# Three-stage attention and two-layer feed-forward kernel: third product's partial sum copied out by ScalarE, decode slots and late jobs moved

## The chip, the cores and the metric

One core of one Trainium2 chip runs the whole program. The metric is device time in microseconds of one execution; lower is better. Engines in the rows: PE is TensorE (PEld its weight loads), DVE is VectorE, ACT is ScalarE, POOL is GpSimd, SP is SyncE, which issues the DMAs.

## The reference, cut to what matters

```
attention, B=8 H=8 S=576 D=64, in chunks of 64:
    p = softmax(q_c @ k_c.T / 8);  x = p @ v_c            -> x [4608, 512]
layer 1:  h = relu(x @ w_in);   g = s*h*h + b;   y   = g @ w_out        (512 -> 2048 -> 512)
layer 2:  h = y @ w2_in;  g = (a0+a1 h+a2 h^2+a3 h^3) / (1+|b0||h|+|b1|h^2+1e-6);  out = g @ w2_out
```

The weights reach the kernel as 64-bit floats and are decoded on the chip.

## The kernel before

The 36 tiles of 128 tokens form ten blocks: 0 and 1 of two tiles, 2 to 9 of four (512 tokens). Blocks 2 to 9 of layer 1 and nine blocks of layer 2 hold nearly all of the time. Every operand is split into a high and a low fp16 half, and a product takes three matmuls (high by high, high by low, low by high).

**Layer 1, blocks 2 to 9** (`l1_group`). A block has four groups, u = 0 to 3, and a group four slots, so a block has 16. A group makes seven products of a fast 2x2 block multiplication ("1", "7", "2", "6", "4", "5", "3", 12 matmuls each, L446) into two PSUM banks called Z and Y, and between them the second matrix product of the group before (`m2(0)` to `m2(3)`, L485) and attention work of the next block. After "4" and "5", Y and Z hold partial sums to which the saved product 7 (`p7`) is added: DVE adds Y+p7 (L519) and Z+p7 (L520) into the tile `h1`. Then ACT makes Relu (L522), Square (L492) and an fp16 copy (L493) of `h1`, and DVE its low half (L494), which is the `g` that the next group's `m2(0)` reads. Product "3" goes on into Z, and ACT reads Z at L527. The next group takes the two banks the other way round: its product 1 goes into the bank that was Y, its product 7 into the one that was Z.

**Other work of a block.** Attention for the next block (scores L264, exponentials, P times V L312, eviction L316 into the single tile `x32`), the seven pieces of x (`x_piece`, L415 on ACT and L416 on DVE), the norm and the seven pieces of y of the block before (`y_norm`, `y_piece`). Scores and P times V share a PSUM bank, so a score waits for the eviction L316 before it, and L316 waits until the last piece of the old `x32` is made.

**Weights of layer 2** are decoded during layer 1 (`w2_load`, `w2_park`): 16 loads of two units each; one unit is three bit operations on DVE (L142, L144, L145), a maximum (L587) and a store to DRAM. `w2_scale` then reduces the maxima over all partitions on POOL and makes the scales; `l2_par(j)` makes the coefficients of layer 2's block j by some twenty one-column DVE operations.

**What sets the order.** `at(slot, job)` gives each job a slot; `run_jobs` issues a slot's jobs inside the group. A scheduling layer then orders the instructions of each engine by readiness and priority, so a job may stand earlier than its slot says. Each engine works its queue in that order.

**Layer 2** is 36 groups; group i makes products into PSUM, group i-1's rational function runs on DVE and ACT (`chain_a` to `chain_e`), and group i-2's second product on PE (L989). `late_jobs` spreads what is left of layer 1 (norm and pieces of the last y block, the last splits of w2_out) over the first groups.

Of the kernel before, what the change touches and what calls it, by code (L numbers as in the profile page):

```python
# [12 lines left out]
AF = mybir.ActivationFunctionType  # L13
ALU = mybir.AluOpType
# [6 lines left out]
def attn_moe_moe2(ctx: ExitStack, tc: tile.TileContext, qk, v, w_in, w_out, s_in, b_in,  # L21
                  w2_in, w2_out, a2_in, b2_in, out):
    nc = tc.nc
# [414 lines left out]
    def product(w, x, u, p, b, start, stop=False):  # L438
        wk, pk = PROD[p]
        for s in range(2):  # L440
            f = 2 * u + s
            for kk in range(2):
                t = w.sh[wk, kk, f // 4]
                for n, (a, l) in enumerate(TERMS):
                    o = (f % 4) * 128
                    T.matmul(out=b[:, s, :], lhsT=t[:, a, o:o + 128], rhs=x[pk][:, l, kk, :],  # L446
                             start=start and s + kk + n == 0, stop=stop and s + kk + n == 4,
                             skip_group_check=True)
# [41 lines left out]
    def l1_half(h, g):  # L490
        hf = h.rearrange("p s b t -> p (s b t)")
        A.activation(out=hf, in_=hf, func=AF.Square)  # L492
        A.activation(out=g[:, 0], in_=hf, func=AF.Copy)  # L493
        V.tensor_tensor(out=g[:, 1], in0=hf, in1=g[:, 0], op=ALU.subtract)  # L494

    def l1_group(j, u, jobs_at, m2):
        x = xhl[j]
        bank = lambda nm: ps_h.tile([128, 2, 256], F32, name=nm, tag="h")
        half = lambda: l1_p.tile([128, 2, 2, 256], F32, name="h1", tag="h1")
        jobs_at(0, crit.get("h"))  # L500
        Z, Y = bank("bZ"), bank("bY")
        product(wi1, x, u, "1", Z, True)
        product(wi1, x, u, "7", Y, True)
        p7 = l1_p.tile([128, 2, 256], F32, name="sn", tag="sn", bufs=3)
        A.activation(out=p7, in_=Y, func=AF.Copy)
        c = A.activation(out=Y, in_=Z, func=AF.Copy)
        m2(0)
        jobs_at(1, c)
        product(wi1, x, u, "2", Y, False)
        product(wi1, x, u, "6", Z, False)  # L510
        h0, h1 = half(), half()
        g = gq[j, u] = g_p.tile([128, 2, 2, 1024], F16, name="g", tag="g")
        A.activation(out=h0[:, :, 0], in_=Y, func=AF.Relu, scale=16.0 * C1)
        c = A.activation(out=Y, in_=Z, func=AF.Copy)
        m2(1)
        jobs_at(2, c)
        product(wi1, x, u, "4", Y, False, True)
        product(wi1, x, u, "5", Z, False)
        V.tensor_tensor(out=h1[:, :, 0], in0=Y, in1=p7, op=ALU.add)  # L519
        V.tensor_tensor(out=h1[:, :, 1], in0=Z, in1=p7, op=ALU.add)  # L520
        h1f = h1.rearrange("p s b t -> p (s b t)")
        A.activation(out=h1f, in_=h1f, func=AF.Relu, scale=16.0 * C1)  # L522
        l1_half(h1, g[:, :, 1])
        m2(2)
        jobs_at(3, c)
        product(wi1, x, u, "3", Z, False, True)
        crit["h"] = A.activation(out=h0[:, :, 1], in_=Z, func=AF.Relu, scale=16.0 * C1)  # L527
        l1_half(h0, g[:, :, 0])
        m2(3)
        if u == 3:  # L530
            xhl.pop(j)
# [32 lines left out]
    def y_norm(j2):  # L564
        m = tiny(KD, "ym")
        for dd in range(KD):
            V.tensor_reduce(out=m[:, dd:dd + 1], in_=y32[j2][:, dd, :], axis=AX.X, op=ALU.max,
                            apply_absolute_value=True)
        norm_bound(m, invy[j2], scy, "yn")
        V.tensor_scalar(out=scy, in0=scy, scalar1=0.25, scalar2=None, op0=ALU.mult)  # L570

# [138 lines left out]

    start = [KF * j for j in range(NB + 1)]
    STAG = 4
    WU = (31, 5, 5)
    PV0 = 5
    WS, WP = 24, 4
    XS = (0, 0, 1, 2, 2, 3, 4)
    P0, P1 = 4, (9, 6, 3, 0)
    seq1 = [(0, f) for f in FO[:STAG]]
# [59 lines left out]
        at(max(pos[1, f] + 6, 30 + k), wo1.split, FO.index(f))  # L778
    at(start[2] + 14, l1_bias)
    for n in range(0, 2 * KF, 2):  # L780
        slot = start[2] + WS + WP * n // 2
        at(slot - 5, w2_load, n)
        at(slot, w2_park, n)
    at(start[2] + WS + WP * KF, w2_scale)

    at(start[3], l2_consts)
    at(start[NB - 1] + 2, l2_par, 0)
    at(start[NB - 1] + 3, l2_par, 1)

    if True:  # L790
        A.preload_act_table_set("natural_log_exp_and_others")
# [223 lines left out]
        extra = {}  # L1015

        def late_jobs():
            for fn, args in [fn for slot in sorted(jobs) for fn in jobs.pop(slot)]:
                extra.setdefault(4 + 2 * YORD.index(args[1]) if fn is y_piece else 3, []).append((fn, args))
            for n in range(len(wo2.cut)):  # L1020
                extra.setdefault(n * 2 // len(wo2.cut), []).append((lambda: wo2.split(wo2.cut.pop(0)), ()))

        last_m2 = m2_of(prev)

# [10 lines left out]
        for i in range(N + 2):  # L1035
            cur, c = i < N, i - 1
            sl = (parts if c in (0, N - 1) else full) if 0 <= c < N else []
            if cur:
                j, u = seq[i]
                if u == 1 and 1 < j + 1 < NB2:  # L1040
                    l2_par(j + 1)
                h = hs[i] = l2_p.tile([128, BIG], F32, name="h", tag="h", bufs=2)
                hq = h.rearrange("p (a s b t) -> p a b s t", a=2, s=2, b=2)
                Z, Y = new_bank(i, "Z"), new_bank(i, "Y")
                l2_product(i, "1", Z, True)
                l2_product(i, "7", Y, True)
                if u == 3 and j + 1 < NB2:
                    l2_load(j + 1)
            for x in sl:
                chain_a(c, x)  # L1050
            for x in sl:
                chain_b(c, x)
            run_m4(i, 0)
            if cur:
                C = new_bank(i, "C")
                A.activation(out=C, in_=Z, func=AF.Copy)
                l2_product(i, "2", C, False)
                l2_product(i, "6", Z, False)
            for x in sl:
                chain_c(c, x)  # L1060
                chain_d(c, x)
                if len(sl) > 1:
                    chain_e(c, x)
            run_m4(i, 1)
            if cur:
                snap(i, "u1", Z)
                snap(i, "p7", Y)
                A.activation(out=hq[:, 0, 0], in_=C, func=AF.Copy)
                l2_product(i, "5", Z, False)
                V.tensor_tensor(out=hq[:, 1, 1], in0=Z, in1=sn.pop((i, "p7")), op=ALU.add)  # L1070
                l2_product(i, "4", Y, False, True)
                V.tensor_tensor(out=hq[:, 1, 0], in0=Y, in1=sn.pop((i, "u1")), op=ALU.add)  # L1072
            if len(sl) == 1:
                chain_e(c, sl[0])
            run_m4(i, 2)
            if cur:
                l2_product(i, "3", Z, False, True)
                A.activation(out=hq[:, 0, 1], in_=Z, func=AF.Copy)  # L1078
            run_m4(i, 3)
            for fn, args in extra.pop(i, []):  # L1080
                fn(*args)
# [36 lines left out]
```

## Time and profile before

| | |
|---|---|
| three runs | 1588.49, 1591.56, 1990.98 us; median 1591.56 |
| profiled execution | 1593.58 us, its span 1591.8 us, mean granted clock 0.988 |
| PE busy | 1544.3 us (97%) |
| DVE busy | 1317.2 us (83%) |
| ACT busy | 962.1 us (60%) |
| chain that ended last | PE 62%, DVE 22%, ACT 7%, DMA 4%, issue 4% |

The span is cut by time: attention of the first tiles, blocks 0 and 1 and the first decodes until about 160 us; layer 1's blocks 2 to 9 until about 876 us; layer 2 after that. A row of a timeline is one instruction or a run of like ones: start and length in us, engine, line, operation, operands, and in brackets how long the engine had been idle just before and what released it. A row of the table by stretch gives for each engine its busy time and, in brackets, its instructions, then the granted clock, the DMA share and GB/s.

### The profile page before, as it was taken

How to read it: one execution, taken by the hardware profiler on the slowest of the kernel's cores; microseconds unless marked ns; L12 is line 12 of the kernel's file. 1: busy time of each engine (PE TensorE's matmuls, PEld its weight loads, DVE VectorE, ACT ScalarE, POOL GpSimd, SP SyncE). 2: the span in 40 equal slices, each digit the busy share in tenths (PEclk: the TensorE clock that was granted, in tenths of full speed). 3: DMA queues.
4: the chain of work that ended last, by engine and by line, in shares of the span. 5: the costliest groups of instructions: out<-in, count | busy, mean ns of one | idle time of the engine just before them, and what ended most of it. 6: DMA issues, size and time to landing. Idle time of an engine off the chain costs nothing.

```text
span 1591.8 us, 29579 instructions
## 1 busy us (share of the span) xinstructions
PE 1544.3 (97%) x12501; PEld 1046.6 (66%) x12501; DVE 1317.2 (83%) x1980; ACT 962.1 (60%) x1268; POOL 24.1 (2%) x57
## 2 busy tenths in 40 slices
PE   8999999989999998999999899999999999999998
PEld 6878666656666665666666666666666666666664
DVE  7987878778878788665684999999999989888887
ACT  3565967656666565655675865555656565656564
POOL 0000000000000000000000000000000000000000
PEclk8999999999999999999999999999999999999999
DMA  7722124444534452311133020101010101010000
GB/s 275 281 76 73 47 55 127 160 139 147 152 107 156 137 166 74 87 41 54 46 121 120 14 86 27 47 27 47 27 47 28 47 27 47 28 47 34 27 27 27
DMA packets 86118, 131.43 MB, mean 83 GB/s; under 512 B 39648, under 2 KB 39648, under 8 KB 85984
## 3 DMA queue, kind: packets, MB, share of 16 engines
q1 hardware_dynamic: 85984, 129.53, 25.8%
q8 instruction: 98, 1.61, 0.4%
q14 instruction: 36, 0.29, 0.1%
HBM read 86.77 MB, written 34.34 MB: 76 GB/s over the span
## 4 chain that ended last, share of the span: by engine, by line
PE 62%; DVE 22%; ACT 7%; DMA 4%; issue 4%; POOL 0%; SPq 0%; DVEq 0%; ACTq 0%; POOLq 0%
PE y L989 18%; PE bZ L446 15%; PE y L485 11%; PE bY L446 10%; DMA raw<-in_moe_w_in_dram 2%; PE bC L446 2%; DVE bits L144 2%; PE hp L455 1%; DVE wf L145 1%; PE y L468 1%; DVE e L957 1%; DVE e L977 1%; DVE e L956 1%; DVE v L971 1%; PE sp L264 1%
## 5 line engine op out<-in xcount | busy, mean ns | idle before, releaser
L446 PEld LDWEIGHTS <-whl 128*128 128x128 f16 x5712 | 558.2, 98 | 134.7 <-issue 19.8
L446 PE MATMUL bZ<-xhl,whl 128*128 128x256 f16 x3264 | 404.2, 274 | 10.6 <-DVE h L520 7.4
L989 PE MATMUL y<-whl,g 128*128 128x512 f16 x1728 | 396.3, 379 | 4.6 <-DVE g L978 3.5
L485 PE MATMUL y<-g,whl 128*128 128x512 f16 x1536 | 353.4, 379 | 2.7 <-ACT g L493 1.8
L989 PEld LDWEIGHTS <-g 128*128 128x128 f16 x1728 | 168.6, 98 | 180.4 <-DVE g L978 5.0
L446 PE MATMUL bY<-xhl,whl 128*128 128x256 f16 x2016 | 253.0, 276 | 2.1 <-ACT sn L937 0.7
L485 PEld LDWEIGHTS <-whl 128*128 128x128 f16 x1536 | 150.4, 98 | 156.8 <-issue 3.4
L1078 ACT ACTIVATE h<-bZ 128x512 f32<-128x512 f32 x36 | 21.5, 596 | 224.8 <-PE bZ L446 173.0
L955 DVE SCALAR_TENSOR_TENSOR v<-v,c 128x2048 f32<-128x2048 f32 (+1 forms) x42 | 85.7, 2044 | 33.4 <-ACT v L946 33.4
L494 DVE TENSOR_TENSOR g<-h,g 128x1024 f16<-128x1024 f32 x64 | 78.2, 1221 | 35.9 <-ACT g L493 35.9
L522 ACT ACTIVATE h<-h 128x1024 f32<-128x1024 f32 x32 | 33.8, 1056 | 115.6 <-DVE h L520 115.6
L956 DVE TENSOR_TENSOR e<-e,h 128x2048 f32<-128x2048 f32 (+1 forms) x42 | 83.1, 1981 | 13.8 <-ACT e L947 13.8
L970 DVE SCALAR_TENSOR_TENSOR g<-e,na,r 128x2048 f16<-128x2048 f32 (+1 forms) x42 | 85.7, 2044 | 5.3 <-ACT r L962 2.2
L957 DVE SCALAR_TENSOR_TENSOR e<-e,na,h 128x2048 f32<-128x2048 f32 (+1 forms) x42 | 85.8, 2045 | 0.7
L977 DVE SCALAR_TENSOR_TENSOR e<-e,na,v 128x2048 f32<-128x2048 f32 (+1 forms) x42 | 85.6, 2042 | 0.7
L947 ACT ACTIVATE e<-h,na 128x2048 f32<-128x2048 f32 (+1 forms) x42 | 77.3, 1842 | 11.6 <-DVE g L978 11.6
L971 DVE SCALAR_TENSOR_TENSOR v<-v,g 128x2048 f32<-128x2048 f32 (+1 forms) x42 | 83.2, 1984 | 1.0
L978 DVE TENSOR_TENSOR g<-e,r 128x2048 f16<-128x2048 f32 (+1 forms) x42 | 82.9, 1976 | 0.1
L946 ACT ACTIVATE v<-h,bc 128x2048 f32<-128x2048 f32 (+1 forms) x42 | 73.8, 1759 | 15.0 <-DVE h L1072 13.9
L961 ACT ACTIVATE r<-v,c 128x2048 f32<-128x2048 f32 (+1 forms) x42 | 73.5, 1756 | 2.6 <-DVE v L955 2.6
L962 ACT ACTIVATE r<-r,c 128x2048 f32<-128x2048 f32 (+1 forms) x42 | 73.5, 1758 | 1.0
L492 ACT ACTIVATE h<-h 128x1024 f32<-128x1024 f32 x64 | 67.4, 1053 | 1.0
(189 smaller groups left out, 1820.7 us busy)
## 6 DMA issues: line engine op xcount, KB each, us to landing
qk<-in_qk_dram SPq DMA_DIRECT2D x36, 512.0 KB, 3.7
raw<-in_moe_w_in_dram SPq DMA_DIRECT2D x16, 1024.0 KB, 5.8
raw<-in_moe_w_out_dram SPq DMA_DIRECT2D x16, 1024.0 KB, 5.4
v<-in_v_dram SPq DMA_DIRECT2D x36, 256.0 KB, 2.7
out_dram<-o SPq DMA_DIRECT2D x36, 256.0 KB, 2.1
yd<-yhl SPq DMA_DIRECT2D x27, 256.0 KB, 2.0
xhl<-yd SPq DMA_DIRECT2D x27, 256.0 KB, 2.6
w2din<-wf SPq DMA_DIRECT2D x16, 256.0 KB, 2.0
```

Source lines behind the costliest of these rows:

```text
L446: T.matmul(out=b[:, s, :], lhsT=t[:, a, o:o + 128], rhs=x[pk][:, l, kk, :], start=start and s + kk + n == 0, stop=stop and s + kk + n == 4 ...
L485: T.matmul(out=ybank[j][dd], lhsT=wo1.hl[f][:, o:o + 128], rhs=g[:, l], start=(first and m == 0), stop=(last and m == 2))
L494: V.tensor_tensor(out=g[:, 1], in0=hf, in1=g[:, 0], op=ALU.subtract)
L947: A.activation(out=e, in_=hh, func=AF.Identity, scale=na[:, 3:4], bias=na[:, 2:3])
L955: V.scalar_tensor_tensor(out=v, in0=v, scalar=dlt, in1=v, op0=ALU.add, op1=ALU.mult)
L956: V.tensor_tensor(out=e, in0=e, in1=hh, op=ALU.mult)
L957: V.scalar_tensor_tensor(out=e, in0=e, scalar=na[:, 1:2], in1=hh, op0=ALU.add, op1=ALU.mult)
L970: V.scalar_tensor_tensor(out=g[:, 0], in0=e, scalar=na[:, 0:1], in1=r, op0=ALU.add, op1=ALU.mult)
L971: V.scalar_tensor_tensor(out=v, in0=v, scalar=q0c, in1=g[:, 0], op0=ALU.add, op1=ALU.mult)
L977: V.scalar_tensor_tensor(out=e, in0=e, scalar=na[:, 0:1], in1=v, op0=ALU.add, op1=ALU.subtract)
L978: V.tensor_tensor(out=g[:, 1], in0=e, in1=r, op=ALU.mult)
L989: T.matmul(out=ybank[j][t], lhsT=g[:, a, q, t * 128:(t + 1) * 128], rhs=w[:, l * 512:(l + 1) * 512], start=(u + q == 0 and m == 0), stop=( ...
```

## The change

Four edits. (1) In `l1_group` ACT copies Z (product 5's sum) into `h1`, and DVE then adds `p7` in place, SBUF on SBUF; product 3, which writes Z next, waits for the ACT copy and not for the DVE add. Relu, Square and the rest of that half are issued after the jobs of slot 3. (2) `w2_park` moves from slots 8, 12, 16, ... (every fourth slot from block 3 on, four to a block, blocks 3 to 7) to slots 3, 7 and 10 of a block (three to a block, blocks 3 to 8); `w2_scale` follows in block 8 instead of block 7. (3) `l2_par` for blocks 0, 1 and now 2 in block 9 at slots 10 to 12 instead of 2 and 3; later ones two groups later, one block further ahead. (4) In layer 2 the last y block's norm is spread over groups 8 to 12 and its pieces over 13 to 25 (before: 3, and 4 to 16); the last splits of w2_out go over three groups instead of two.

```diff
         product(wi1, x, u, "5", Z, False)
+        A.activation(out=h1[:, :, 1], in_=Z, func=AF.Copy)
         V.tensor_tensor(out=h1[:, :, 0], in0=Y, in1=p7, op=ALU.add)
-        V.tensor_tensor(out=h1[:, :, 1], in0=Z, in1=p7, op=ALU.add)
-        h1f = h1.rearrange("p s b t -> p (s b t)")
-        A.activation(out=h1f, in_=h1f, func=AF.Relu, scale=16.0 * C1)
-        l1_half(h1, g[:, :, 1])
+        V.tensor_tensor(out=h1[:, :, 1], in0=h1[:, :, 1], in1=p7, op=ALU.add)
         m2(2)
         jobs_at(3, c)
+        h1f = h1.rearrange("p s b t -> p (s b t)")
+        with tc.issue_after(last(nc.scalar.engine)):
+            A.activation(out=h1f, in_=h1f, func=AF.Relu, scale=16.0 * C1)
+        l1_half(h1, g[:, :, 1])
         product(wi1, x, u, "3", Z, False, True)
...
+    PARK = [start[j] + o for j in range(3, 9) for o in (3, 7, 10)][1:17]
-    WS, WP = 24, 4
...
-        slot = start[2] + WS + WP * n // 2
+        slot = PARK[n // 2]
...
-    at(start[2] + WS + WP * KF, w2_scale)
+    at(PARK[-1] + 3, w2_scale)
...
-    at(start[NB - 1] + 2, l2_par, 0)
-    at(start[NB - 1] + 3, l2_par, 1)
+    for j in range(3):
+        at(start[NB - 1] + 10 + j, l2_par, j)
...
         def late_jobs():
-            for fn, args in [fn for slot in sorted(jobs) for fn in jobs.pop(slot)]:
-                extra.setdefault(4 + 2 * YORD.index(args[1]) if fn is y_piece else 3, []).append((fn, args))
+            m = tiny(KD, "ym")
...
+            for dd in range(KD):
+                extra.setdefault(8 + dd, []).append((y_max, (dd,)))
+            extra.setdefault(12, []).append((y_bound, (NB2 - 1, m)))
+            for n, p in enumerate(YORD):
+                extra.setdefault(13 + 2 * n, []).append((y_piece, (NB2 - 1, p)))
+            jobs.clear()
             for n in range(len(wo2.cut)):
-                extra.setdefault(n * 2 // len(wo2.cut), []).append((lambda: wo2.split(wo2.cut.pop(0)), ()))
+                extra.setdefault(n * 3 // len(wo2.cut), []).append((lambda: wo2.split(wo2.cut.pop(0)), ()))
...
-                if u == 1 and 1 < j + 1 < NB2:
-                    l2_par(j + 1)
+                if u == 3 and 3 <= j + 2 < NB2:
+                    l2_par(j + 2)
```

The order on DVE where the last group of block 4 begins, right behind the third group's add of Z (`bits` and `wf` are a decode, `g` the low half that the next m2 reads). Before:

```order
L520 TENSOR_TENSOR h_5226<-bZ,sn 128x2x256
L142 TENSOR_SCALAR bits<-raw 128x512
L144 SCALAR_TENSOR_TENSOR bits<-raw,bits 128x512
L145 SCALAR_TENSOR_TENSOR wf<-raw,bits 128x512
L587 TENSOR_REDUCE am_226<-wf 128x1
L494 TENSOR_TENSOR g<-h_5226,g 128x1024
L317 TENSOR_REDUCE xmx<-x_4400 128x4
L244 TENSOR_SCALAR xsc<-inv 128x1
L402 TENSOR_TENSOR tx<-x_4400 128x512
```

and now:

```order
L521 TENSOR_TENSOR h_5220<-h_5220,sn 128x2x256
L494 TENSOR_TENSOR g<-h_5220,g 128x1024
L317 TENSOR_REDUCE xmx<-x_4404 128x4
L244 TENSOR_SCALAR xsc<-inv 128x1
L402 TENSOR_TENSOR tx<-x_4404 128x512
```

The decode that stood between the add and the low half is gone. At the end of the same group, before:

```order
L106 TENSOR_SCALAR ape<-apm 128x1
L287 RECIPROCAL rs<-sm 128x8
L108 TENSOR_SCALAR inv<-ape 128x1
L145 SCALAR_TENSOR_TENSOR wf<-raw,bits 128x512
L519 TENSOR_TENSOR h_5541<-bY,sn 128x2x256
L109 RECIPROCAL sc<-inv 128x1
L288 TENSOR_TENSOR e<-e,rs 128x512
L520 TENSOR_TENSOR h_5541<-bZ,sn 128x2x256
L587 TENSOR_REDUCE am_226<-wf 128x1
```

and now:

```order
L520 TENSOR_TENSOR h_5534<-bY,sn 128x2x256
L106 TENSOR_SCALAR ape<-apm 128x1
L285 TENSOR_SCALAR sm<-sm 128x8
L145 SCALAR_TENSOR_TENSOR wf<-raw,bits 128x512
L108 TENSOR_SCALAR inv<-ape 128x1
L287 RECIPROCAL rs<-sm 128x8
L109 RECIPROCAL sc<-inv 128x1
L592 TENSOR_REDUCE am_226<-wf 128x1
L521 TENSOR_TENSOR h_5534<-h_5534,sn 128x2x256
L288 TENSOR_TENSOR e<-e,rs 128x512
```

Between the adds of Z of the third and the fourth group stand two whole decodes where there were three, the third of them up to its maximum; and the product L288 stands behind the add. The same holds for blocks 3 to 6; block 7, which had no decode there, now has the same two.

The order on ACT at the end of that block's third group (`h_5226` and `h_5220` are h1, `h_5225` and `h_5219` the other half). Before:

```order
L522 ACTIVATE h_5226<-h_5226 128x1024
L492 ACTIVATE h_5226<-h_5226 128x1024
L493 ACTIVATE g<-h_5226 128x1024
L316 ACTIVATE x_4400<-xp,xsc 128x4x128
L527 ACTIVATE h_5225<-bZ 128x2x256
```

and now:

```order
L519 ACTIVATE h_5220<-bZ 128x2x256
L526 ACTIVATE h_5220<-h_5220 128x1024
L492 ACTIVATE h_5220<-h_5220 128x1024
L493 ACTIVATE g<-h_5220 128x1024
L316 ACTIVATE x_4404<-xp,xsc 128x4x128
L529 ACTIVATE h_5219<-bZ 128x2x256
```

The copy of Z stands in front; behind it the order is as it was, and the read of product 3's Z (L529) still stands behind Relu, Square and Copy of h1.

The order on DVE at `w2_scale`: before, in the first group of block 7:

```order
L641 TENSOR_REDUCE w2m<-am_226 128x2
L494 TENSOR_TENSOR g<-h_7973,g 128x1024
L96 TENSOR_SCALAR w2pm<-w2x 128x2
L98 TENSOR_SCALAR w2pe<-w2pm 128x2
L99 TENSOR_SCALAR w2i<-w2pe 128x2
```

and now, in the second group of block 8:

```order
L646 TENSOR_REDUCE w2m<-am_226 128x2
L96 TENSOR_SCALAR w2pm<-w2x 128x2
L98 TENSOR_SCALAR w2pe<-w2pm 128x2
L99 TENSOR_SCALAR w2i<-w2pe 128x2
L100 RECIPROCAL w2s<-w2i 128x2
```

`w2x` is POOL's result; the operation that stood between the reduction and its reader is now behind it, and the one-column operations of two `l2_par` follow in the same group, as before.

## Rows read from the trace of the kernel before

**Rows 1.** Table by stretch: layer 1's blocks 2 to 9, the change to layer 2.
```profile
160.00:876.00 716.00, 695.09 (x6533) 463.62 (x6532) 536.18 (x1162) 457.59 (x685) 19.47 (x41) 0.99 0.36 108
876.00:1060.00 184.00, 173.54 (x1178) 114.50 (x1176) 176.63 (x169) 115.28 (x120) 0.74 (x1) 1.00 0.12 38
```

**Rows 2.** Timeline of PE: its waits from block 3's end to block 7.
```profile
332.66 1.47 PE L446 MATMUL bZ<-xhl,whl 128*128 128x256 f16 x12 [3.30 <-DVE h L520]
...
343.27 0.68 PE L264 MATMUL sp<-qk 64*64 64x64 f32 x18 [1.39 <-ACT x L316]
...
422.66 1.47 PE L446 MATMUL bZ<-xhl,whl 128*128 128x256 f16 x12 [1.26 <-DVE h L520]
...
433.27 0.68 PE L264 MATMUL sp<-qk 64*64 64x64 f32 x18 [1.38 <-ACT x L316]
...
510.65 1.47 PE L446 MATMUL bZ<-xhl,whl 128*128 128x256 f16 x12 [0.92 <-DVE h L520]
...
521.26 0.68 PE L264 MATMUL sp<-qk 64*64 64x64 f32 x18 [1.39 <-ACT x L316]
...
600.72 1.47 PE L446 MATMUL bZ<-xhl,whl 128*128 128x256 f16 x12 [1.33 <-DVE h L520]
...
614.13 1.12 PE L264 MATMUL sp<-qk 64*64 64x64 f32 x18 [4.19 <-ACT x L316]
```

**Rows 3.** Table by stretch of 25 us: those with a fallen clock after these waits.
```profile
325.00:350.00 25.00, 20.32 (x191) 13.23 (x189) 21.09 (x41) 14.06 (x23) 0.68 (x1) 0.93 0.50 156
...
500.00:525.00 25.00, 22.69 (x208) 14.84 (x207) 22.05 (x46) 14.32 (x23) 0.56 (x1) 0.94 0.57 185
...
600.00:625.00 25.00, 20.09 (x153) 13.82 (x153) 22.20 (x103) 11.98 (x18) 1.69 (x2) 0.93 0.32 101
```

**Rows 4.** Timeline of PE over a group of block 4 without waits.
```profile
373.97 1.47 PE L446 MATMUL bZ<-xhl,whl 128*128 128x256 f16 x12
...
378.84 1.48 PE L446 MATMUL bZ<-xhl,whl 128*128 128x256 f16 x12
...
381.46 1.47 PE L446 MATMUL bZ<-xhl,whl 128*128 128x256 f16 x12
382.77 1.47 PE L446 MATMUL bY<-xhl,whl 128*128 128x256 f16 x12
...
395.21 1.47 PE L446 MATMUL bZ<-xhl,whl 128*128 128x256 f16 x12
```

**Rows 5.** Timeline of all engines at block 4's end.
```profile
416.46 1.47 PE L446 MATMUL bZ<-xhl,whl 128*128 128x256 f16 x12
...
421.33 0.67 DVE L288 TENSOR_TENSOR e<-e,rs 128x512 f32<-128x512 f32 x1
421.92 0.68 DVE L520 TENSOR_TENSOR h<-bZ,sn 128x512 f32<-128x512 f32 x1
...
422.64 1.06 ACT L522 ACTIVATE h<-h 128x1024 f32<-128x1024 f32 x1 [5.43 <-DVE h L520]
...
423.12 0.41 DVE L142 TENSOR_SCALAR bits<-raw 128x512 int32<-128x512 int32 x1
...
425.02 0.69 DVE L587 TENSOR_REDUCE am<-wf 128x1 f32<-128x512 f32 x1
```

**Rows 6.** Groups by line, whole span: an ACT copy of a PSUM bank.
```profile
L514 ACT ACTIVATE bY<-bZ 128x512 f32<-128x512 f32 x32 | 18.6, 582 | 18.7 <-PE bZ L446 18.4
```

**Rows 7.** Timeline of DVE around `w2_scale` and two `l2_par`, between two adds of Z.
```profile
599.98 0.68 DVE L520 TENSOR_TENSOR h<-bZ,sn 128x512 f32<-128x512 f32 x1
...
603.80 0.19 DVE L641 TENSOR_REDUCE w2m<-am 128x2 f32<-128x32 f32 x1
...
605.45 0.17 DVE L96 TENSOR_SCALAR w2pm<-w2x 128x2 f32<-128x2 f32 x1 [0.26 <-POOL w2x L643]
...
626.03 0.68 DVE L520 TENSOR_TENSOR h<-bZ,sn 128x512 f32<-128x512 f32 x1
```

**Rows 8.** Waits of PE from 880 to 1060 us: total, times, longest.
```profile
PE y L989 <- DVE g L978: 3.5, 5, 1.0
```

More of the change, by code (lines that the diff above doesn't have):

```diff
@@ L568, in y_norm, with y_bound @@
                             apply_absolute_value=True)
+        y_bound(j2, m)
+    def y_bound(j2, m):
         norm_bound(m, invy[j2], scy, "yn")
@@ L1017, in late_jobs, with y_max @@
         def late_jobs():
-            for fn, args in [fn for slot in sorted(jobs) for fn in jobs.pop(slot)]:
-                extra.setdefault(4 + 2 * YORD.index(args[1]) if fn is y_piece else 3, []).append((fn, args))
+            m = tiny(KD, "ym")
+            def y_max(dd):
+                V.tensor_reduce(out=m[:, dd:dd + 1], in_=y32[NB2 - 1][:, dd, :], axis=AX.X, op=ALU.max,
+                                apply_absolute_value=True)
+            for dd in range(KD):
[4 more added lines that the diff above has]
+            jobs.clear()
             for n in range(len(wo2.cut)):
-                extra.setdefault(n * 2 // len(wo2.cut), []).append((lambda: wo2.split(wo2.cut.pop(0)), ()))
+                extra.setdefault(n * 3 // len(wo2.cut), []).append((lambda: wo2.split(wo2.cut.pop(0)), ()))
         last_m2 = m2_of(prev)
```

## The prediction

> **What bounds the kernel now.** I read the page first: PE is busy 97% of the span, so the only time to be had is what PE spends waiting or at half clock. The table by stretch says where that is [rows 1]: layer 1's blocks leave PE idle 716.0 - 695.1 = 20.9 us, the first 184 us of layer 2 leave 184.0 - 173.5 = 10.5 us, with DVE busy 176.6 of those 184 us. The timeline of PE then gives the places in layer 1 [rows 2]: a pair of waits at each change of block from 3 to 4 up to 6 to 7. The first of a pair is product 3 of a block's last group, waiting for DVE to add out of Z (3.30, 1.26, 0.92, 1.33: 6.81 us); about 10 us later a score waits for an eviction by ACT, which itself waits for DVE's last pieces of x (1.39, 1.38, 1.39, 4.19: 8.35 us). Together 15.16 us, all of it from a DVE that is late. The changes from block 7 to 8 and 8 to 9, with no decodes around them, have no such pair. Third, the granted clock falls to 0.93 to 0.94 of a 25 us stretch after three of the four pairs [rows 3]: 1.2 instead of 2.4 GHz for a piece of it, which is 25 x 0.07 = 1.75 us of work lost each time, 5.25 us in all. The price list of the waits is therefore 20.4 us in layer 1 and 10.5 at layer 2's start, and the change can hardly win more than that.
>
> **How late DVE is, and what is moved.** In a group without waits [rows 4], counted from the start of product 5, product 3 starts 4.87 us later, the next group's product 1 after 7.49, its product 7 after 8.80, and the next product 5 after 21.24. At block 4's end [rows 5] product 5 started at 416.46 and DVE's add of Z ran from 5.46 to 6.14 us after it; product 3 was due at 4.87, and 6.14 - 4.87 = 1.27 is the wait that the timeline shows.
>
> *The ACT copy of Z.* Product 3 now needs an ACT copy instead of the DVE add. A copy of a PSUM bank costs 0.58 us [rows 6]; ACT stood idle 5.43 us in front of its Relu at this very place [rows 5], and over layer 1 it is busy 458 of 716 us [rows 1], so 32 x 0.58 = 18.6 us more of it lie in idle time. What this buys is less than it seems. The order on ACT shows that the read of product 3's Z still stands behind Relu, Square and Copy, and all of them behind DVE's add. That read frees the bank for the next group's product 7. Three ACT operations of 1.06 us, the read of 0.58 and some 0.1 us of handing over make 3.9 us, so the add must be finished by 8.80 - 3.9 = 4.9 us: the same as product 3's 4.87 before. The wait is passed on, not taken away; by itself I cost this edit at nothing, in either direction. Its cover is ACT's idle time before Relu; if ACT reached the copy more than 4.87 - 1.3 - 0.6 = 3.0 us late, product 3 would wait again.
>
> The Trainium skill, "ScalarE: Activation LUTs", section "Rules for kernel authors", would leave such plain elementwise work to VectorE, as up to three times faster there in bf16. The rows show the opposite for this fp32 tile out of PSUM: 0.58 us on ACT beside 0.68 for the add on DVE [rows 5, 6]. By the page's ratio the copy would take an estimated 2.0 us, no group without lateness would yet wait, but 1.4 us of its slack would be gone in all 32 groups, and the slower rival below would be the likelier.
>
> *The decodes.* This is where I see the gain. Between the last two adds of Z of blocks 3 to 6 DVE has one decode less up to its maximum: 423.12 to 425.02, 1.9 us [rows 5]; and L288 (0.67) now stands behind the add: 2.5 us together. At block 4's end the add would finish at 6.14 - 2.5 = 3.6 us, inside 4.9; so at blocks 5 and 6, whose waits were alike. At block 3's end, 2.04 us later, 5.7: about 0.8 remains. Block 7 gets the decodes of blocks 4 to 6 and should, like them, just not wait. I put 1.0 us for what is left over. The pieces of x follow at once, with fewer decodes before them and starting 2.5 us earlier; the score's waits of 1.38 and 1.39 are shorter than that and go. The stores and loads of the decodes on SP's queue move with them and remain behind transfers that are not waited for on PE.
>
> *`w2_scale` and `l2_par`.* The 4.19 us wait lies in the group in which these run: between its two adds of Z DVE needed 626.03 - 599.98 = 26.05 us [rows 7] where PE needs 21.24. The order shows the same mass of one-column operations again, in block 8's second group. There the reader of POOL's result stands right behind the reduction; the result took 605.45 - 603.80 - 0.19 = 1.46 us, of which DVE idled only 0.26, so 1.2 us of idling come back: 27.3 us. DVE comes out 27.3 - 21.24 = 6.0 us late, of which some 2.3 us are slack (the add starts at 1.95, behind the copy, and may start at 4.2); 3.7 us of waiting by this, 4.5 with the part of a y norm that now shares the group. So 4.19 goes and 4.5 comes, with half a fall of the clock, 0.9.
>
> *Layer 2's start.* Two of the eight splits and the later coefficients move out of the first groups, but the scheduler pulls the last y block's pieces forward again: in the order they stand one group later than before, not nine. Of PE's waits for DVE there, 3.5 us for `g` [rows 8] within 10.5 us of idle time, I take 3.0; ends 0 and 5.9.
>
> *The clock.* All three falls go with their waits: 5.25 us. The rows show falls after waits as short as 1.39 us following 0.92 us eleven us before, and none after 1.38 following 1.26 [rows 2, 3]. The Trainium skill, "TensorE: Matmul & The Clock Gate", section "Why this matters for your kernels", lays a fall in mid-kernel to one long idle stretch. By that only the falls after 3.30 and 4.19 us would hang on these waits, 3.5 us instead of 5.25; I go by the rows.
>
> **The sum**, against the profiled execution's own 1593.6 us (span 1591.8 and 1.8 around it): -15.2 (waits) - 5.25 (clock) + 1.0 (left over) + 4.5 + 0.9 (block 8) - 3.0 (layer 2) = -17.0, 1576.6 us. The profiled run stood 2.0 above the median of the runs, 1591.6, so I say **1575 us** for the median, 1.0% less. Bounds of the terms: block 8 free and layer 2 at 5.9 gives -26 and 1565.5; a remainder of 1.5 us at each of five block ends, a whole fall in block 8 and nothing in layer 2 gives about -7 and 1584.
>
> **Rivals.**
> 1. *The wait only changes its name.* DVE's lateness at the block ends comes not from the decodes but from its waits inside the queue, for raw weights and for ACT's results, and product 7 then waits where product 3 did. For it: DVE was busy only 21 to 22 of 25 us in those stretches [rows 3], so something besides work held it. Against it: blocks 7 and 8 run without a wait. Half of the 15.2 stays, the clock falls too, block 8 costs its 5.4: -7.6 + 5.4 - 1.5 = about -4, 1588 us. Chance 0.20.
> 2. *Slower: the copy stands behind ACT's waits.* ACT works in order; if in groups with a decode the exponential or a piece in front of the copy waits for DVE, then product 3, the add, Relu and product 7 all wait. It decides from 3.0 us of lateness of the copy on. With 1.5 us in each of the 20 groups of blocks 3 to 7 (30 us) and four falls (7), against 20.4 + 3.0 gained and 5.4 for block 8: +19, 1610 us. Against it: ACT is idle at that place. Chance 0.08.
> 3. *Nothing waits in block 8.* The 2.3 us of slack and DVE's idle time take up `w2_scale`, and layer 2's start gains all 5.9: -26, 1565 us. Chance 0.10.
> My forecast, 1566 to 1584: 0.62.
>
> **Range.** 1565 to 1590 holds the forecast, most of rival 1 and half of rival 3. Two per cent, about what a measurement tells from no change, is 32 us: 1559.7 would need all of the price list and more, 0.03; above 1623, 0.02; within, 0.95.
>
> **What the profile after would show.** No wait of product 3 on DVE at the block ends, and scores there that wait for nothing; if products 1 or 7 of the next group wait in their place, rival 1. A wait of 3 to 5 us near the middle of block 8, with DVE full of one-column operations, or none (rival 3). ACT copies of 0.6 us that start within 1 us of product 5's end, or late ones (rival 2). In layer 2 the waits for `g` before 1060 us more than halved. I am wrong if layer 1's idle time of PE stays above 15 us.

## The result, and the profile after

The changed kernel takes **1604.72 us** (median of 4 runs, 1602.87 to 1605.95) against 1590.73 before: ratio 1.0092, 95% interval [1.0072, 1.0112]. It is 0.9% slower, where 1.0% faster was forecast, and outside the range. Timed once more among the experiments it was 1600.91, ratio 1.0070 [1.0054, 1.0087]. One of the four runs of before, of 1990.98 us, was disturbed and is left out of the ratio, though not of the 1590.73 (the other three have the median 1589.90).

The profiled execution after has a span of 1603.3 us, 11.5 more than before's 1591.8, with the same mean granted clock of 0.988. The waits of PE over the whole span, three groups of them (us in total, times, longest):

```profile
PE bY L446 <- ACT h L529: 21.4, 16, 3.3
PE sp L264 <- ACT x L316: 11.8, 8, 3.0
PE y L994 <- DVE g L983: 3.5, 5, 1.0
```

The first is new: product 7 waits for ACT's read of product 3's Z, which was L527 before and released a single wait of 0.5 us. Product 3's waits on DVE (7.4 us before) are gone. The scores' (11.8 us before) and layer 2's (3.5 us before) did not shrink. The table by stretch, to be read against [rows 1] (layer 1's blocks 2 to 9 now end near 888 us):

```profile
160.00:888.00 728.00, 696.44 (x6530) 462.69 (x6530) 533.96 (x1161) 473.51 (x716) 21.34 (x41) 0.99 0.35 106
888.00:1072.00 184.00, 174.87 (x1186) 115.24 (x1185) 175.08 (x169) 116.20 (x122) 0.67 (x1) 1.00 0.12 39
```

Layer 1 leaves PE idle 31.6 us instead of 20.9, the start of layer 2 9.1 instead of 10.5. So the loss is in layer 1. Where it is, the timeline of PE shows; these answer to [rows 2], now for blocks 4, 5 and 8:

```profile
384.72 1.47 PE L446 MATMUL bY<-xhl,whl 128*128 128x256 f16 x12 [1.70 <-ACT h L529]
...
427.53 1.47 PE L446 MATMUL bY<-xhl,whl 128*128 128x256 f16 x12 [0.17 <-ACT h L529]
...
434.39 0.68 PE L264 MATMUL sp<-qk 64*64 64x64 f32 x18 [1.55 <-ACT x L316]
...
474.84 1.47 PE L446 MATMUL bY<-xhl,whl 128*128 128x256 f16 x12 [1.99 <-ACT h L529]
...
519.95 1.47 PE L446 MATMUL bY<-xhl,whl 128*128 128x256 f16 x12 [2.47 <-ACT h L529]
...
526.81 0.68 PE L264 MATMUL sp<-qk 64*64 64x64 f32 x18 [1.54 <-ACT x L316]
...
750.43 2.48 PE L446 MATMUL bY<-xhl,whl 128*128 128x256 f16 x12 [2.35 <-ACT h L529]
```

Three places are to be seen. **Behind the second group of a block** (384.72, 474.84) product 7 waits 1.7 to 2.0 us, where nothing waited before; over blocks 3 to 7 this is 3.33 + 1.70 + 1.99 + 2.30 + 1.89 = 11.2 us. **At a block's end** (427.53, 519.95) product 7 waits 0.23, 0.17, 2.47, 0.42 and 0.17 us, 3.5 in all, in place of product 3's 6.8. **About 7 us after that** a score waits (434.39, 526.81), five times 1.55 us.

Why the second group is late, the timeline of DVE in block 4 shows, from its idle time in front of a decode to the add of Z:

```profile
374.80 0.43 DVE L142 TENSOR_SCALAR bits<-raw 128x512 int32<-128x512 int32 x1 [1.73 <-DMA raw<-in_moe_w_in_dram]
...
375.99 0.68 DVE L288 TENSOR_TENSOR e<-e,rs 128x512 f32<-128x512 f32 x1
...
376.67 0.68 DVE L144 SCALAR_TENSOR_TENSOR bits<-raw,bits 128x512 int32<-128x512 int32 x1
377.25 0.69 DVE L520 TENSOR_TENSOR h<-bY,sn 128x512 f32<-128x512 f32 x1
377.86 0.68 DVE L145 SCALAR_TENSOR_TENSOR wf<-raw,bits 128x512 int32<-128x512 int32 x1
378.45 0.69 DVE L408 TENSOR_TENSOR tx<-y 128x512 f32<-128x512 f32 x1
379.06 0.68 DVE L592 TENSOR_REDUCE am<-wf 128x1 f32<-128x512 f32 x1
379.65 0.69 DVE L521 TENSOR_TENSOR h<-h,sn 128x512 f32<-128x512 f32 x1
```

A decode now stands in the second group ahead of the add. DVE, which works its queue in order, first idles 1.73 us for the decode's raw weights and then makes the decode. The add ends at 380.34. PE and ACT at the same place:

```profile
374.06 1.47 PE L446 MATMUL bZ<-xhl,whl 128*128 128x256 f16 x12
```

```profile
380.37 1.06 ACT L526 ACTIVATE h<-h 128x1024 f32<-128x1024 f32 x1 [4.21 <-DVE h L521]
381.46 1.06 ACT L492 ACTIVATE h<-h 128x1024 f32<-128x1024 f32 x1
382.55 1.06 ACT L493 ACTIVATE g<-h 128x1024 f16<-128x1024 f32 x1
383.51 0.67 ACT L316 ACTIVATE x<-xp,xsc 128x512 f32<-128x512 f32 x1
384.08 0.59 ACT L529 ACTIVATE h<-bZ 128x512 f32<-128x512 f32 x1
```

The row of PE is product 5. The add ends 380.34 - 374.06 = 6.28 us after its start, where the prediction's rule asks for 4.9. Product 7 waits 1.70 us: the 1.38 of that, and a part of the eviction L316 (0.67) that stands in the way. The rule held; it was applied to the last groups alone.

The one long wait at a block's end, 2.47 us in block 5, has the same row in front of it on DVE:

```profile
504.79 0.43 DVE L142 TENSOR_SCALAR bits<-raw 128x512 int32<-128x512 int32 x1 [2.22 <-DMA raw<-in_moe_w_out_dram]
```

The two waits go together in blocks 3 to 7. In front of the decode DVE waits for raw weights 3.16, 1.73, 1.49, 2.33 and 1.71 us in the second groups, where product 7 then waits 3.33, 1.70, 1.99, 2.30 and 1.89; in the last groups it is 0, 0, 2.22, 0.17 and 0 us, against 0.23, 0.17, 2.47, 0.42 and 0.17. In b0 and f1 below, which have the copy and the same slots, the two also lie within 0.51 us of each other in each of these ten places. So in these three traces it is the wait for the load, more than the decode's own work, that product 7 waits out; no run takes the load's wait away and leaves all else as it is.

### The profile page after: what moved, and what is told of

Read it like the earlier page. It is cut to its first block, busy times and chain, and to the rows that moved or that the text cites. A ratio compares the mean times of both kernels' runs of the same rounds, so it can differ in the third digit from the quotient of the medians.

```text
span 1603.3 us, 29625 instructions
## 1 busy us (share of the span) xinstructions
PE 1546.1 (96%) x12501; PEld 1045.9 (65%) x12501; DVE 1314.8 (82%) x1980; ACT 978.4 (61%) x1300; POOL 25.9 (2%) x57
## 4 chain that ended last, share of the span: by engine, by line
PE 54%; DVE 24%; ACT 12%; DMA 5%; issue 4%; POOL 1%; SPq 0%; DVEq 0%; POOLq 0%; ACTq 0%
PE y L994 19%; PE bZ L446 13%; PE bY L446 9%; PE y L485 7%; ACT h L492 2%; PE bC L446 2%; DMA raw<-in_moe_w_out_dram 2%; ACT g L493 2%; DVE bits L144 2%; DVE wf L145 2%; ACT h L526 2%; DMA raw<-in_moe_w_in_dram 2%; PE hp L455 1%; PE y L468 1%; ACT y L550 1%
## 5 line engine op out<-in xcount | busy, mean ns | idle before, releaser
L494 DVE TENSOR_TENSOR g<-h,g 128x1024 f16<-128x1024 f32 x64 | 78.2, 1223 | 57.5 <-ACT g L493 57.5
L526 ACT ACTIVATE h<-h 128x1024 f32<-128x1024 f32 x32 | 33.8, 1055 | 63.9 <-DVE h L521 63.9
L493 ACT ACTIVATE g<-h 128x1024 f16<-128x1024 f32 x64 | 67.4, 1055 | 0.8
```

## The experiments

Each kernel was timed in rounds beside the kernel before on the same chip; ratios are to that, with a 95% interval. "Idle" is PE's idle time in the 480 us from 280 to 760 us of the span, which holds most of blocks 3 to 8: 16.2 before, 25.1 after. It is that of one profiled execution; those of c1 (1592.1 us) and f2 (1591.2) lie well below their medians.

| kernel | us, median | ratio | idle |
|---|---|---|---|
| a1 copy and later Relu alone | 1593.54 | 1.0014 [0.9999, 1.0030] | 14.4 |
| a2 slots alone | 1592.33 | 1.0015 [0.9999, 1.0032] | 20.0 |
| a3 layer 2 edits alone | 1589.74 | 0.9988 [0.9974, 1.0003] | 15.5 |
| a4 all but copy and later Relu | 1591.44 | 1.0002 [0.9987, 1.0017] | 19.2 |
| b0 the change again | 1600.91 | 1.0070 [1.0054, 1.0087] | 23.3 |
| b1 read of product 3 early | 1602.43 | 1.0084 [1.0069, 1.0099] | 14.0 |
| b2 raw weights loaded once | 1594.59 | 1.0031 [1.0018, 1.0045] | 15.9 |
| b3 decodes behind the add | 1587.76 | 0.9986 [0.9976, 0.9995] | 12.5 |
| c1 pieces of x earlier | 1599.71 | 1.0055 [1.0036, 1.0074] | 17.9 |
| c2 decodes clear, pieces earlier | 1581.04 | 0.9938 [0.9922, 0.9954] | 8.3 |
| f1 the change, Relu where it was | 1599.79 | 1.0058 [1.0039, 1.0077] | 24.0 |
| f2 the change, no copy | 1595.14 | 1.0025 [1.0004, 1.0046] | 18.9 |
| d1 before, pieces of x earlier | 1586.64 | 0.9970 [0.9957, 0.9982] | 17.0 |
| d2 as c2, no copy, no later Relu | **1567.68** | **0.9854** [0.9839, 0.9869] | 0.6 |
| d3 as c2, units two slots apart | 1577.33 | 0.9914 [0.9900, 0.9929] | 6.9 |
| d4 as d3, one slot later | 1595.09 | 1.0027 [1.0014, 1.0040] | 17.6 |
| e1 d2 with the copy | 1579.54 | 0.9930 [0.9905, 0.9955] | 9.7 |
| e2 d2 with the later Relu | 1569.91 | 0.9869 [0.9836, 0.9902] | 0.3 |

**The four parts apart.** Theory T1: the wait is passed on, and the moved decodes make the loss. T2: the first edit makes it. T3: the layer 2 edits do.

a1, the first edit alone:

```diff
+        A.activation(out=h1[:, :, 1], in_=Z, func=AF.Copy)
-        V.tensor_tensor(out=h1[:, :, 1], in0=Z, in1=p7, op=ALU.add)
+        V.tensor_tensor(out=h1[:, :, 1], in0=h1[:, :, 1], in1=p7, op=ALU.add)
```

> The kernel before with the first edit alone (ACT copies Z, DVE adds in place, Relu/Square/Copy issued after slot 3's jobs). Theory T1 (the wait is only passed on; the loss comes from the moved decodes): same as before, 1591 us +-3; product 3's 7.4 us of waits on DVE go, product 7 waits 6 to 10 us for ACT's read L529 at the same block ends. Theory T2 (the first edit itself makes the loss, as the add now stands behind one more ACT step and product 7's wait is longer than product 3's was): 1598 us or more, product 7 waits over 15 us.

a2, the slots alone:

```diff
-        slot = start[2] + WS + WP * n // 2
+        slot = PARK[n // 2]
```

> The kernel before with the second edit alone (decodes at slots 3, 7, 10, w2_scale in block 8). T1: the second groups are late here too, and product 3 waits for DVE's add there: 1602 us +-3, product 3's waits on DVE 12 to 20 us. T2: the slots are harmless or good by themselves: 1592 us or less, product 3's waits under 8 us.

a3, the third and fourth edits:

```diff
-    at(start[NB - 1] + 2, l2_par, 0)
+        at(start[NB - 1] + 10 + j, l2_par, j)
```

> The kernel before with the third and fourth edits alone (l2_par later, last y norm and pieces spread further). T1 and T2: layer 2's start gains the 1.7 us seen between the two traces, 1589 us +-2. Theory T3 (the moved layer 2 work makes the loss): 1598 us or more.

a4, the change with the first edit undone:

```diff
-        A.activation(out=h1[:, :, 1], in_=Z, func=AF.Copy)
+        V.tensor_tensor(out=h1[:, :, 1], in0=Z, in1=p7, op=ALU.add)
```

> The changed kernel without its first edit. T1: the same loss under another name, 1603 us +-3, with product 3 waiting for DVE in the second groups where product 7 waits in the changed kernel. T2: the loss is gone, 1592 us or less.

No part alone loses more than 0.15% (none is clear of no change), and together they lose 0.7 to 0.9%. T1 is right on a1 and wrong on a2 and a4 (1602 and 1603 expected), T3 is wrong on a3. T2 is right on a4 and wrong on a1; on a2 its time came out to 0.3 us, but product 3 waits 11.0 us for DVE there, not under 8. What loses is the first edit in the new slots. The waits of a4 from 250 us on show that the second groups are late there too:

```profile
PE bZ L446 <- DVE h L520: 7.8, 5, 2.8
PE sp L264 <- ACT x L316: 5.0, 5, 1.4
```

Behind the second groups of blocks 3 to 7 product 3 waits for the add where product 7 does in the change, with 0.25 us of product 7 behind it: 8.8 us in all, against 11.2. The scores wait 5.0 us instead of 7.7, and the clock falls twice after 280 us instead of three times.

**What holds product 7.** The change again, and three edits of it:

> The changed kernel once more, beside the kernels of this call, since the four parts taken alone or without the first edit lay within 2.4 us of before. If the loss is the kernel's own: 1604 us +-3, ratio to before 1.007 to 1.010. If it came from where it was measured: 1593 us or less.

b1, ACT's read of product 3 ahead of Square and Copy:

```diff
+        product(wi1, x, u, "3", Z, False, True)
+        crit["h"] = A.activation(out=h0[:, :, 1], in_=Z, func=AF.Relu, scale=16.0 * C1)
         l1_half(h1, g[:, :, 1])
-        product(wi1, x, u, "3", Z, False, True)
-        crit["h"] = A.activation(out=h0[:, :, 1], in_=Z, func=AF.Relu, scale=16.0 * C1)
```

> The changed kernel with ACT's read of product 3 (L529) issued right behind Relu, ahead of Square and Copy of the first half. Theory Q (product 7 waits because that read stands behind three ACT operations that wait for DVE's late add): the 21 us of product 7 fall below 8 us, second products wait for g some 5 us at most, 1592 us +-4. Rival W (DVE is simply late with the add, and whoever is next on the chain waits as long): the second product waits for ACT's copy of g 15 us or more, 1603 us +-4.

b2, no reload of raw weights:

```diff
+        if n == 0:
+            w.load(i, raw_p, "raw")
-        w.load(i, raw_p, "raw")
+        w.raw[w.order[i]], w.raw[w.order[i + 1]] = keep
```

> The changed kernel with the raw weights of layer 2 loaded once and every decode reading that same tile (leaves out 15 of the 16 loads, so layer 2 works with wrong weights). Theory D (Z's add is late because DVE, in order, is held in front of it by the decode's load, 1 to 3.7 us each, 21 us in all): product 7's waits in the second groups of blocks 3 to 7 fall from 1.7 to 3.3 us to under 0.8, 1592 us +-4. Rival W2 (the lateness is DVE's work, not its waits): they stay over 1.2 us each, 1601 us +-4.

b3, each decode behind the DVE instruction before it:

```diff
-for o in (3, 7, 10)][1:17]
+for o in (3, 7, 11)][1:17]
-        at(slot - 5, w2_load, n)
+        at(slot - 3, w2_load, n)
+            with tc.issue_after(last(nc.vector.engine)):
                 w.decode(i, raw_p, "wf")
```

> The changed kernel with decode slots 3, 7, 11, loads three slots ahead of each decode instead of five, and each decode issued behind the DVE instruction before it in the program, so that most of it stands behind Z's add. D and Q: Z's add comes on time in the second groups, product 7 waits under 8 us in all, 1588 us +-4. Rival: the low half of g and the pieces of x come later instead, second products or scores wait, 1598 us or more.

The loss repeats (b0). In b1 product 7's waits fall to 4.2 us, but the second product now waits for both halves of g, 10.2 + 10.1 us (over a third of it outside the stretch of the table): rival W in its time, though ACT's half is 10.1 us and not 15. An early read moves the wait once more. Over the whole span PE's idle time is 52.4 us in b1 and 57.2 after, so its profile does not show all of what makes it as slow. b2 says less than it was built for: without loads to wait for, the scheduler drew all 32 decodes forward to between 256 and 433 us. Product 7 waits there, and from 465 us to block 9 not at all; where the decodes are, the waits are, but the share of the loads is not separated. In b3 the waits behind the second groups are gone, and 0.8% of the change's time with them. But its edit does two things at once: the decodes stand behind the add, and DVE no longer waits for raw weights in front of any of them (24.5 us in the change from 240 us on, none in b3, c2, d2, d3, e1 and e2). Which of the two does it, b3 does not tell apart. What is left from 250 us on:

```profile
PE sp L264 <- ACT x L316: 7.8, 5, 1.6
PE bY L446 <- ACT h L529: 7.0, 9, 1.6
```

So the score's waits do not come with the late adds. ACT in b3, at a block's end, up to the eviction that the score waits for (until 339.42, 1.55 us):

```profile
331.92 0.58 ACT L529 ACTIVATE h<-bZ 128x512 f32<-128x512 f32 x1
...
334.57 1.05 ACT L493 ACTIVATE g<-h 128x1024 f16<-128x1024 f32 x1
...
337.15 0.71 ACT L415 ACTIVATE xhl<-x,c 128x512 f16<-128x512 f32 x1
338.68 0.69 ACT L316 ACTIVATE x<-xp,xsc 128x512 f32<-128x512 f32 x1 [0.82 <-DVE xhl L416]
```

The last piece of x (L415 at 337.15) stands behind the whole chain of the group, and the eviction into the single `x32` waits for it.

**The pieces, and the halves of the first edit.**

c1, the change with the last two pieces one slot earlier:

```diff
-    XS = (0, 0, 1, 2, 2, 3, 4)
+    XS = (0, 0, 1, 2, 2, 2, 3)
```

> The changed kernel with the last two pieces of x one slot earlier (XS 2, 3 for 3, 4). Theory S (the score's wait of 1.55 us at every change of block comes from the last piece of x standing late in ACT's queue, behind Relu, Square and Copy, and it brings the falls of the clock there): the score's 11.8 us fall below 4, falls of the clock at block ends from three to at most one, 1592 us +-4; product 7's waits stay near 20 us. Rival: the score waits for something else (the shared bank or the tile itself), its waits stay over 8 us and the time within 2 us of the changed kernel's.

c2, b3 with that and other slots:

```diff
-for o in (3, 7, 11)][1:17]
+for o in (0, 4, 8)][1:17]
```

> Decodes behind Z's add (as in the run before it), now at slots 0, 4, 8 so that none falls into a block's last group, and the pieces of x one slot earlier. If the second groups' waits come from decodes in front of the add and the score's from the late piece: product 7 waits under 5 us in all, the score under 4, 1578 us +-4, faster than before by 0.8%. Rival: DVE's work itself, which is the same, is what is late: a wait of the same size shows up elsewhere (g, scores, pieces), 1588 us or more.

f1 (copy kept, Relu where it was) and f2 (no copy, Relu later), both on the change:

```diff
 f1: A.activation(out=h1f, in_=h1f, func=AF.Relu, ...) back ahead of m2(2)
 f2: V.tensor_tensor(out=h1[:, :, 1], in0=Z, in1=p7, ...) back, no AF.Copy
```

> The changed kernel with Relu, Square and Copy issued where they were before (right behind the adds), the ACT copy kept. If the loss of the first edit with the new slots comes from the copy: 1603 us +-3. If it comes from the later issue of Relu (behind slot 3's jobs, L316 ahead of them): 1593 us +-3.

> The changed kernel without the ACT copy (DVE adds out of Z as before), the later issue of Relu kept. The mirror of the run before: if the copy makes the loss 1592 us +-3, if the later issue makes it 1603 us +-3.

c1: the score's waits at the block ends are gone in the profile (one of 2.8 us near the start is left), as S said, but its median is only 1 to 5 us below the change's two, not the 9 or more expected (its ten runs lie between 1592.1 and 1603.5, and the profile is of the fastest). c2 is 0.6% faster than before, within the range expected, but product 7 still waits 1 to 2 us behind each second group of blocks 3 to 7, 11.9 us in the whole span and not under 5. f1 is 1.0058, f2 1.0025, each just outside the range expected if the copy makes the loss and far from the other: the copy is the larger half.

**The two open points.** d1 is the kernel before with c1's edit alone; d2 is c2 with the first edit undone (a4's diff); d3 and d4 take c2's two units of a decode two slots apart:

```diff
         at(slot, w2_park, n)
+        at(slot + 2, w2_park, n + 1)
```

> The kernel before with only the last two pieces of x one slot earlier. Theory S (score's waits at block ends come from those pieces' place in ACT's queue, not from the decodes): the score's 8.4 us at the four block ends go and the time falls by 5 to 10 us, 1584 us +-3, product 3's waits staying. Rival (DVE's lateness at block ends sets both waits, as the prediction had it): the waits move to product 3, 7 or g, 1591 us +-3.

> The kernel with all adds clear of decodes and pieces earlier, without the ACT copy and the later Relu. If the copy costs by itself in every schedule (some 8 us in the slots of the changed kernel): 1573 us +-3. If it costs only where DVE is late, and is neutral or good once the add is on time: 1581 us or more.

> The same kernel with the copy, and the two units of a decode two slots apart (slots 0 and 2, 4 and 6, 8 and 10). DVE has less work in one piece in front of the second group's add, and does not wait for the first unit's store: product 7's waits in the second groups, 1.1 to 2.0 us each, fall to under 1, 1577 us +-3. Rival: the scheduler packs them together again, 1581 us +-2.

> As the run before, with slots 1 and 3, 5 and 7, 9 and 11. Every decode stands behind the low half of g or a piece of it, none between the adds: product 7's waits in the second groups under 0.8 us each, 1575 us +-3. Rival: the raw loads, now issued later too, hold DVE in front of the next group's add: 1583 us or more.

d1: ratio 0.9970. The score's 8.4 us go but for 0.5, and product 3 waits 15.4 us from 250 us on instead of 7.4. The pieces do set the score's wait, as S says, but the rival is right on where it goes: all of it turns up at product 3 (idle in the stretch of the table is 17.0 us, 16.2 before). What the 4 us are made of, this profile shows only in part: its clock does not fall near 170 and 230 us, as before's does. d3: 1577.33, as expected, but the second groups' waits fell below 1 us in three blocks only (1.90 and 2.40 in the others). d4: 1595.09: its rival came true, DVE waits for raw weights again (12.5 us from 240 us on, 1.7 to 3.9 us at a time).

d2 is the surprise, below both ranges: 1567.68, 1.5% faster than before and 2.1% faster than the change (by b0's ratio). Its table by stretch for blocks 3 to 8, then those of c2, of before and of the change:

```profile
280.00:760.00 480.00, 479.36 (x4649) 318.62 (x4647) 374.94 (x862) 308.43 (x460) 11.95 (x31) 1.00 0.38 116
```

```profile
280.00:760.00 480.00, 471.66 (x4621) 312.44 (x4619) 371.96 (x865) 309.91 (x466) 15.15 (x31) 1.00 0.40 118
```

```profile
280.00:760.00 480.00, 463.79 (x4531) 308.75 (x4529) 365.17 (x842) 290.56 (x435) 14.25 (x31) 0.99 0.39 117
```

```profile
280.00:760.00 480.00, 454.91 (x4418) 301.01 (x4417) 358.35 (x833) 295.20 (x448) 15.92 (x31) 0.99 0.39 117
```

PE is busy 479.36 of 480 us and its clock does not fall: all that this stretch had to give, taken with the add straight out of PSUM. In block 9, behind the stretch, PE now waits some 5 us for DVE and ACT, where it waited 1.7 before.

**Which half of the first edit, and how.** e1 is d2 with the copy, e2 is d2 with the later Relu (f1's and f2's diffs).

> The fastest kernel so far (adds clear of decodes, pieces earlier, no first edit) with the ACT copy put back, Relu issued right behind the adds as there. In this order DVE makes both low halves of g of a block's first group ahead of the decode; without the copy the decode stands between them. If the copy makes the 13 us between the two kernels by that: 1580 us +-3, product 7 waits 1 to 2 us in each second group. If the later issue of Relu makes them: 1569 us +-3, no waits there.

> The mirror: the fastest kernel with only the later issue of Relu, DVE adding out of Z. Its order on DVE has the decode between the two low halves. If the copy makes the loss 1569 us +-3; if the later issue makes it 1580 us +-3.

e1: 1579.54, PE idle 9.7 us in the stretch. e2: 1569.91, idle 0.3. It is the copy. Their two profiles, with the same mean granted clock of 0.992, are 1578.5 and 1568.7 us long; 43.7 - 35.8 = 7.9 of these 9.8 us are idle time of PE. All pairs that differ by one half:

| with the add | without either | copy | later Relu | both |
|---|---|---|---|---|
| in the change's slots | 1.0002 | 1.0058 | 1.0025 | 1.0070, 1.0092 |
| clear of decodes | 0.9854 | 0.9930 | 0.9869 | 0.9938 |
| in the slots before | 1 | | | 1.0014 |

The copy costs 0.45 to 0.76% in every pair of the first two rows; the later Relu's 0.1 to 0.3% are not clear of the intervals. The order on DVE in block 4's first group suggests how. With the copy (c2):

```profile
349.22 0.69 DVE L521 TENSOR_TENSOR h<-h,sn 128x512 f32<-128x512 f32 x1 [1.25 <-ACT h L519]
351.70 0.69 DVE L569 TENSOR_REDUCE ym<-y 128x1 f32<-128x512 f32 x1 [1.79 <-ACT y L550]
...
357.61 0.69 DVE L569 TENSOR_REDUCE ym<-y 128x1 f32<-128x512 f32 x1 [0.93 <-ACT y L550]
358.21 0.68 DVE L402 TENSOR_TENSOR tx<-y 128x512 f32<-128x512 f32 x1
358.81 1.22 DVE L494 TENSOR_TENSOR g<-h,g 128x1024 f16<-128x1024 f32 x1
...
360.61 0.42 DVE L142 TENSOR_SCALAR bits<-raw 128x512 int32<-128x512 int32 x1
...
373.54 0.68 DVE L521 TENSOR_TENSOR h<-h,sn 128x512 f32<-128x512 f32 x1
```

and without (d2):

```profile
340.86 0.68 DVE L520 TENSOR_TENSOR h<-bZ,sn 128x512 f32<-128x512 f32 x1
344.42 0.69 DVE L567 TENSOR_REDUCE ym<-y 128x1 f32<-128x512 f32 x1 [2.88 <-ACT y L548]
...
348.41 0.42 DVE L142 TENSOR_SCALAR bits<-raw 128x512 int32<-128x512 int32 x1
...
350.67 1.22 DVE L494 TENSOR_TENSOR g<-h,g 128x1024 f16<-128x1024 f32 x1
...
363.87 0.68 DVE L520 TENSOR_TENSOR h<-bZ,sn 128x512 f32<-128x512 f32 x1
```

The add itself waits 1.25 us for the copy. With the copy all four maxima of y (L569) and both low halves of g (L494) then stand ahead of the decode; without it, two of the maxima (L567) and the first low half. The decode begins 11.4 us after the add (360.61 - 349.22) against 7.6 (348.41 - 340.86). Product 5 of the second group, in c2 and in d2:

```profile
368.32 1.47 PE L446 MATMUL bZ<-xhl,whl 128*128 128x256 f16 x12
```

```profile
360.15 1.47 PE L446 MATMUL bZ<-xhl,whl 128*128 128x256 f16 x12
```

The second group's add ends 374.22 - 368.32 = 5.9 us after product 5 began, against 364.55 - 360.15 = 4.4 in d2. The limit is 4.9: product 7 waits 1.32 us in c2, and nothing in d2. This order is the scheduler's, made anew for each kernel. No run has the copy with d2's order, so whether the copy costs by what DVE waits for or by the order that the scheduler makes around it is not shown.

## Why the prediction was wrong

- **The sum.** -17.0 us forecast, +11.5 found in the span: at block ends -6.8 + 3.5; second groups +11.2; scores 8.35 before, 5 x 1.55 = 7.75 after, -0.6; block 8 +2.35; block 9 +0.5 (2.2 us after, 1.7 before); layer 2's start -1.3; clock 0. These make 8.9 of the 9.7 us by which PE's idle time grew (57.2 after, 47.5 before); for 1.8 us more it was busy.
- **The step that failed: "The decodes. This is where I see the gain."** At the block ends 6.8 us of waits became 3.5, where 1.0 was forecast; 2.47 of the 3.5 is block 5's end, which was to be inside the 4.9. And the decodes taken out of the last groups went into the second ones, and those were not followed: +11.2. The rule of 4.9 us for the end of the add, which the prediction had, gives their waits when it is put beside the row of the add. The decode was priced by its work (1.9 us), and its loads were said to "remain behind transfers that are not waited for on PE"; DVE waits for them in front of the add, and PE for DVE. Without the first edit this step gives neither gain nor loss (a4, 1.0002): it is the forecast gain that did not come.
- **The second step that failed, and the loss itself: the ACT copy, "by itself I cost this edit at nothing, in either direction".** In the old slots that is within the interval (1.0014, [0.9999, 1.0030], both halves). In the change's slots, and in those of c2, it costs 0.45 to 0.76%, 7 to 12 us. It was priced by ACT's idle time (true: product 3 found it done, the copy starts 0.04 us after product 5 in 29 of 32 groups) and by PE's path (true); not by DVE, which waits for it in order (11.4 us in the change) and whose queue is arranged around it. The Trainium skill, "ScalarE: Activation LUTs", section "Rules for kernel authors", has add, mul and the like on VectorE. The outcome agrees; not its reason, speed, as the copy is the shorter instruction here (0.60 us in c2 at this place, the add out of Z 0.68 in d2).
- **The scores, "shorter than that and go".** They stayed, because the last piece of x stands behind ACT's chain, and not, as the prediction had it, because DVE is late. Earlier pieces took them away in d1, c1, c2 and d2; alone (d1) they sent the wait to product 3, and the 0.3% by which d1 is faster is not explained.
- **The clock, -5.25.** From 280 to 760 us there are three falls as before, one again at block 6's end and two elsewhere. Stretches of 10 us of the change (the first fall runs on into the next stretch, at 0.95):

```profile
610.00:620.00 10.00, 8.28 (x71) 5.31 (x71) 4.90 (x7) 6.13 (x10) 0.00 (x0) 0.88 0.80 150
710.00:720.00 10.00, 10.00 (x60) 6.42 (x59) 5.99 (x18) 2.92 (x6) 0.83 (x1) 0.84 0.33 126
750.00:760.00 10.00, 9.57 (x55) 6.07 (x55) 5.10 (x7) 6.30 (x10) 0.00 (x0) 0.83 0.28 79
```

  A fall to 1.2 GHz takes 10 x 0.17 = 1.7 us. The first follows waits of 0.42 and 1.55 us, the second of only 0.17 and 1.55, each pair seven us apart, the third one of 2.35. By the Trainium skill, "TensorE: Matmul & The Clock Gate", section "Why this matters for your kernels", a drop in mid-kernel comes from one long idle stretch between matmuls; this trace disagrees: in front of these three falls stand only the waits named.
- **Right:** block 8 (one wait of 2.35 us in its second group, 4.5 forecast, and a fall of 1.7 us behind it, 0.9 forecast); no wait of product 3 on DVE; rival 2 out, as the copies were on time. **Rival 1** named the mechanism, product 7 in product 3's place, gave the wait for raw weights as its cause, and kept it at the block ends: 1588 us instead of 1604.7. "I am wrong if layer 1's idle time of PE stays above 15 us": it is 31.6. The lower bound was added up wrongly: -17.0 with block 8's 5.4 taken out and 2.9 more in layer 2 is -25.3, not -26; it changes nothing here.

What stays open: no run separates the wait for the load from the decode's own work, since b2 and b3 moved both; that the one makes nearly all of the lateness rests on their going together in three traces. With the copy gone (a4) it is not one to one: DVE waits 3.85, 3.40, 3.70, 2.99 and 3.73 us for raw weights there, PE 2.8, 1.3, 2.1, 0.9 and 1.7. Why the copy costs that slack is open too.

## What to carry to other kernels

When work moves out of a late place, follow it to where it lands, and put the same deadline to that place. An engine that works in order is late by what stands in front of the instruction that matters, its waits included, so keep loads' consumers and other movable work behind it: in b3, where this also ended the waits for the loads, it took away 0.8% of the change's time, and the fastest kernel here (d2) has it and no copy. Handing a read to an idle engine adds a dependency, and it is not free just because both engines have idle time.

## What the runs showed of the hardware

The granted clock fell or not under the same waits: in b3 five equal pairs of waits (0.64 us, then 1.55 seven us later) were followed by a fall in three cases. Near 100 us, in a part that no kernel here changes, it fell in some profiles (before, after) and not in others (a4, d2). A fall is 1.7 us in most places and twice that in some (near 100 us before and after). Ten runs of one kernel lie 5 to 14 us apart (31 of before 10 and 11, 4 of d2 4).
